# The router's count of preceding tokens: a running sum on VectorE and two products on TensorE instead of one product a unit, with the first stage planned anew

## The chip, the cores and the metric

The kernel runs on one core of a Trainium2 chip. The core has five engines with queues of their own: TensorE (PE in the profile; its weight loads are PEld), VectorE (DVE), ScalarE (ACT), GpSimd (POOL) and SyncE (SP, which here only issues transfers). The metric is device time in microseconds for one execution.

## What is computed

Two layers, one after the other. The first is a DeltaNet attention: 4 batches, 8 heads, 768 positions, head size 48. Each head keeps a 48x48 state and walks along the positions:

```python
k_n = k / (norm(k) + 1e-6)
for t in range(S):
    y[:, :, t] = q_t @ state
    v_old = state.T @ k_t
    state = state + b_t * outer(k_t, v_t - v_old)
```

The result, as 3072 rows of 384, goes into a mixture of 8 experts with a noisy router:

```python
noisy = x @ w_gate + log1p(exp(x @ w_noise)) * noise
top2 = the two largest of 8; weights = softmax over these two
for e in range(8):
    out[rows of e] += weight * (relu(x[rows of e] @ w1[e]) @ w2[e])
```

All numbers are float32; `w1[e]` is 384x1024 and `w2[e]` is 1024x384.

## The kernel before

The first stage (`deltanet`, up to about 356 us in the profile) works in chunks of 64 positions. A unit is one chunk of two batches, 128 rows; a step `s` (0 to 5) is four units (`US`). Within a chunk the recurrence becomes matrix products with the inverse of a triangular matrix. The names that matter:

- `products` (L630, with the transposes L614) makes the Gram matrices of the keys. ScalarE or VectorE copies their diagonal blocks out (L663, L669), and VectorE transposes them (L680).
- `invert` inverts the blocks of one to three steps at once, on VectorE: a scaling (L749), then 30 pairs of column operations (L761 and L765), then a scaling (L777). The groups are `INVERSIONS`: step 0, steps 1 and 2, steps 3 and 4, step 5. `end_inversion` transposes the result (L788, L796), and `join` puts it together with copies on ScalarE (L819, L853, L857) and products (L839, L845).
- `within` makes the masked product of queries and keys, `qk` (L882).
- `recur` and `answer` walk through the units. GpSimd scales `v` (L912), TensorE multiplies keys and state (L630), VectorE subtracts (`v`, L932), TensorE solves (L948), ScalarE copies `u`, TensorE gathers the new state (L970), VectorE adds it (L982); TensorE makes the answer (L903, L1007), which is stored, transposed (L1017) and multiplied with the router's weights (L1022).

The router (`route`) runs three times (`ROUTES`): after step 2 for 12 units, after step 4 for 8, and after step 5 for 4. VectorE finds the two experts of each token; `taken` is a 128 x units x 8 table of zeros and ones. Each token then needs the number of earlier tokens with the same expert, which is its row in that expert's list. `count_earlier` makes this in PSUM: one product with a strictly triangular matrix counts within the unit (L1144), a product with `ones` for each shift by one unit or more adds the preceding units of the run (L1146), and a last one adds `before`, the counts of the preceding runs (L1150). `rows` turns the count into addresses, and `spread` scatters a token's number, weight and place to its list in DRAM, by one indirect transfer per unit and choice on GpSimd (L441). `counted` brings `before` up to date (L1171).

When a part of expert 0's list is there, its rows are gathered (`early_rows`, L1283 and L405) and computed already in the first stage (`early`, L1327 to L1384), for five tiles of 128 rows. Then the expert stage begins: `rest` does what is left of expert 0, and seven experts follow, with products that are saved by sums of blocks (`PLAN`, L1596). This stage is written in a fixed order and isn't touched by the change, but for line numbers.

The order of the first stage is made by a planner when the kernel is built. `Jobs.add` takes each piece of work with its engine, a cost, what it reads and writes, and perhaps a due time; `order` plays the jobs through and takes, engine by engine, among those that could start at about the same moment, the one due first. What comes out is the instruction order of each engine's queue, and it is fixed: at run time an engine waits for the instruction at the head. The constants below bear on this:

- `FIRST`, `PACE`, `BEHIND` give the due times of each step; `SOONER` moves those of `rows`.
- `AFTER` is added to the due time of the scatters, `APART` is their distance.
- `PATIENCE` is how much later a more urgent job may start and still be preferred; `SOON` makes jobs due that hold a PSUM bank.
- `EASY` (one number for each router run) multiplies the time that the planner allows for results of the router's steps to reach another engine (`lands`).

Of the kernel before, what the change touches and what calls it, by code (L numbers as in the profile page):

```python
# [11 lines left out]
ALU = mybir.AluOpType  # L12
ACTF = mybir.ActivationFunctionType
AX = mybir.AxisListType
# [13 lines left out]
EARLY_TILES = 5  # L28
WEIGHTS = 300.0
WITHIN = {}  # L30
EASY = 0.4, 0.4, 0
SOONER = 10, 40, -40
PUT_IN_RULE = -1
ROWS = TILES * 128 + MORE
# [2 lines left out]
ROUTES = [(0, 3), (3, 2), (5, 1)]  # L37


FIRST, PACE, BEHIND = 15, 44, 165  # L40
INVERSIONS = [(0, 1), (1, 2), (3, 2), (5, 1)]


# [57 lines left out]
class Jobs:  # L101
# [45 lines left out]
    def order(self):  # L147
# [28 lines left out]
        while len(done) < len(jobs):  # L176
            first = {}
            best = None
            for engine in self.ENGINES:
# [12 lines left out]
                if at:  # L192
                    soon = min(at)[0] + self.PATIENCE
                    pick = min((x for x in at if x[0] <= soon), key=lambda x: x[1:])
# [7 lines left out]
            if job.opens:  # L202
# [4 lines left out]
                for y in job.opens.users:  # L207
                    if jobs[y].late is None:
                        jobs[y].key = 0, min(jobs[y].due, end + self.SOON)
            if job.closes:  # L210
# [12 lines left out]
                    could[jobs[j].engine].add(j)  # L223
        return sorted(done, key=lambda job: job.start)

    AFTER = 20
    APART = 1.6
    PATIENCE = 0.014
    SOON = 32

    def run(self):

# [5 lines left out]
def kernel(  # L238
# [39 lines left out]
    nc = tc.nc  # L278
# [3 lines left out]
    E = moe_w_gate.shape[1]  # L282
# [22 lines left out]
        out=mask_u, in_=mask_u, pattern=[[1, 128]], base=0, channel_multiplier=-1,  # L305
# [18 lines left out]
    ones = const.tile([128, 128], FP32, name="ones")  # L324
# [20 lines left out]
    before = const.tile([128, E], FP32, name="before")  # L345
# [124 lines left out]
    def deltanet(ictx):  # L470
# [4 lines left out]
        jobs = Jobs(  # L475
            [psum.tile([128, 512], FP32, name=f"single{i}") for i in range(2)],
            [psum.tile([128, 2, 512], FP32, name=f"pair{i}") for i in range(3)],
        )
        PE, ACT, DVE, POOL, SP = Jobs.ENGINES

        def bank(size, ahead=False):

            if size == 2:
                return Bank(2, (0, 1) if ahead else (0, 1, 2))
            return Bank(1, (0,) if ahead else (0, 1))

        def sb(shape, name, dtype=FP32):
            return pool.tile(shape, dtype, name=name)

        def ring(shape, name, n, zero=None, engine=nc.gpsimd):  # L490

            made = [sb(shape, f"{name}{i}") for i in range(n)]
            for t in made:
                for part in zero(t) if zero else ():
                    engine.memset(part, 0.0)
            return lambda i: made[i % n]
# [24 lines left out]
        WIDE = max(x for _, x in ROUTES) * US  # L521
# [550 lines left out]
            for x in ("top0", "top1", "expert0", "expert1", "p1", "den", "row")  # L1072
        }
        metas = ring([128, WIDE, 2, META], "meta", 2)
        r_count = sb([128, E], "r_count")
        slots = [[sb([128, WIDE], f"slot{i}_{x}", I32) for x in range(2)] for i in range(2)]

        def route(g):
# [4 lines left out]
            s, units = first_s + steps - 1, steps * US  # L1083
            u, w, d, noisy, hit0, hit1, taken, at = (x[:, 0:units] for x in full.values())
# [7 lines left out]
            p = bank(1)  # L1092

            def vv(out, a, b, op):
                nc.vector.tensor_tensor(out=out, in0=a, in1=b, op=op)  # L1095
# [46 lines left out]
            def count_earlier():  # L1142
                p_at = p.tile[:, 0 : units * E].rearrange("p (u e) -> p u e", e=E)
                nc.tensor.matmul(p_at, mask_u, taken, start=True, stop=False)  # L1144
                for i in range(1, units):
                    nc.tensor.matmul(  # L1146
                        p_at[:, i:], ones, taken[:, 0 : units - i],
                        start=False, stop=False, skip_group_check=True,
                    )
                nc.tensor.matmul(  # L1150
                    p_at, ones, before[:, None, :].to_broadcast([128, units, E]),
                    start=False, stop=True,
                )

            def rows():
                p_at = p.tile[:, 0 : units * E].rearrange("p (u e) -> p u e", e=E)
# [10 lines left out]
                nc.vector.reciprocal(gate0, den)  # L1167
                vv(gate1, p1, gate0, ALU.mult)

            def counted():  # L1170
                nc.vector.tensor_reduce(  # L1171
                    out=r_count, in_=taken.rearrange("p u e -> p e u"), axis=AX.X, op=ALU.add
                )
                vv(before, before, r_count, ALU.add)

            looked_up = [("early_meta", lo) for x in EARLY if x < first_s for lo, _ in EARLY[x][:1]]
            every_logit = [("logits", g % 2, i) for i in range(units)]
# [11 lines left out]
                writes=[("num", g % 2)],  # L1189
            )  # L1190


            easy = lambda x: x * EASY[g]
            jobs.add(
# [4 lines left out]
                lands=easy(4.0),  # L1199
# [4 lines left out]
                writes=["r_w", "r_noisy"],  # L1204
# [6 lines left out]
                writes=["r_u", "r_hit1", "r_p1", "r_taken"], lands=easy(4.0),  # L1211
            )
            jobs.add(
                PE, 0.3 + 0.28 * units, count_earlier, reads=["r_taken", "before"], opens=p,
                lands=easy(2.0),
            )
            jobs.add(ACT, 0.25, lambda: nc.scalar.activation(p1, p1, ACTF.Exp), writes=["r_p1"])
# [2 lines left out]
                writes=["r_at", "r_d", "r_row", ("slot", g % 2)], closes=p,  # L1220
                due=FIRST + s * PACE + BEHIND - SOONER[g],
            )
            jobs.add(DVE, 0.9, weights, reads=["r_p1"], writes=["r_den", meta])
            jobs.add(DVE, 0.4, counted, reads=["r_taken"], writes=["before"])
            for x in range(units):
                of, i = first_s + x // US, x % US
                for y, to in enumerate(slot):
# [5 lines left out]
                        reads=[("slot", g % 2), meta, ("num", g % 2), "blank", *looked_up],  # L1233
                        writes=[("rows", of, i, y)], lands=2.0, moves=0.2,
                        due=FIRST + (s + paced) * PACE + BEHIND + jobs.AFTER,
                        apart=jobs.APART * paced,
# [197 lines left out]
        for s in range(NS):  # L1434
            units = range(s * US, (s + 1) * US)
            g = inversion_of[s]
            if s == INVERSIONS[g][0]:
# [7 lines left out]
                for x in range(s, s + INVERSIONS[g][1]):  # L1445
                    for j, cost, moves, emit, writes in large.get(x, ()):
                        jobs.add(
                            SP, cost, emit, writes=writes, lands=2.0, moves=moves,
                            reads=[("column", x, j)],
                        )  # L1450
            end_inversion(s)
            if s + 1 == NS:
                jobs.add(
                    SP, 0.7, lambda: nc.sync.dma_start(out=w1_even, in_=w1r[0]), lands=2.0,
                    writes=[
                        "w1", ("t", 0),
                        *(("gd", i, lo) for i in range(US) for lo in range(0, 128, Q)),
                    ],
# [4 lines left out]
                    writes=["w2", ("t", 1)], moves=5.5, due=WEIGHTS + 20.0,  # L1463
# [9 lines left out]
            if s + 1 == sum(ROUTES[turn_r]):  # L1473
                route(turn_r)
# [12 lines left out]
    with ExitStack() as ictx:  # L1487
        weights, early_puts = deltanet(ictx)
# [371 lines left out]
    with tc.If(count > ROWS):  # L1860
        for e in range(E):
            with tc.tile_pool(name=f"left{e}", bufs=1) as pool:
                w1e, w2e = load_weights(weight_tiles(pool), e)
                earlier, added = added, []
                for i in range(TILES, NT):
# [19 lines left out]
                    for fo in range(FT):  # L1885
                        p_h = psum.tile([128, 128], FP32, name="p_hl")
                        for do in range(KT):
                            nc.tensor.matmul(
                                p_h, w1e[:, do, fo * 128 : (fo + 1) * 128], xe[:, do],
                                start=(do == 0), stop=(do == KT - 1),  # L1890
# [40 lines left out]
```

## Time and profile before

| | us |
|---|---|
| three timed runs | 837.17, 839.2, 845.06 |
| median | 839.2 |
| the profiled execution | 798.04 |
| its span, from first to last instruction | 796.2 |

| engine | busy, us | share of the span | instructions |
|---|---|---|---|
| TensorE | 712.5 | 89% | 9361 |
| TensorE weight loads | 559.4 | 70% | 9361 |
| VectorE | 537.6 | 68% | 1079 |
| ScalarE | 309.2 | 39% | 728 |
| GpSimd | 417.6 | 52% | 408 |

The profile is of one execution. Busy shares are averages over two stages that differ, so the text reads windows and chains: the slices cut the span in 40, each digit being the busy tenths of one, and PEclk the clock granted to TensorE in tenths of full speed. The mean granted clock over the whole execution was 0.906. In the chain of waits each line is a start, a duration and the work that ended last. One float32 product of the program is two matmul records.

### The profile page before, as it was taken

To read this page: it belongs to the slowest core of one execution; us is meant where nothing else is said; L and a number is where in the kernel's file an instruction comes from. 1 tells how busy PE (TensorE), PEld (TensorE's weight loads), DVE (VectorE), ACT (ScalarE), POOL (GpSimd) and SP (SyncE) were. 2 spreads that over 40 slices of the span, in tenths; PEclk is the share of its full clock that TensorE was granted. 3 is DMA by queue.
4 is the path that set the end of the run, shared out by engine and by line. 5 is a ranking of instruction groups with operands and counts; after the bars stand their busy time and mean duration, and the time that the engine had idled before them with its cause. 6 is when DMAs were issued, how large, how long until landed. Compare 5 with 4: busy or idle time off the path is not lost.

```text
span 796.2 us, 22454 instructions
## 1 busy us (share of the span) xinstructions
PE 712.5 (89%) x9361; PEld 559.4 (70%) x9361; DVE 537.6 (68%) x1079; ACT 309.2 (39%) x728; POOL 417.6 (52%) x408
## 2 busy tenths in 40 slices
PE   4656878788878889999999999999999999999993
PEld 3445767677768778766597597597596596696693
DVE  7899969999971243016786785785885884884831
ACT  3658387758646432212511511502502602502500
POOL 5021021110255345588886796786787787786032
PEclk8556786977787699999999999999999999999997
DMA  3457553412544213358346346355355345423031
GB/s 66 82 103 191 143 138 78 89 41 60 147 75 122 62 30 127 99 125 165 120 140 130 87 139 133 86 137 126 93 137 118 103 126 118 110 43 42 0 41 25
DMA packets 142719, 79.60 MB, mean 100 GB/s; under 512 B 118352, under 2 KB 139024, under 8 KB 141584
## 3 DMA queue, kind: packets, MB, share of 16 engines
q1 hardware_dynamic: 125840, 57.25, 27.4%
q0 software_dynamic: 12800, 19.80, 13.5%
q8 instruction: 75, 1.23, 0.7%
q10 hardware_dynamic: 3968, 1.03, 0.6%
q14 instruction: 36, 0.29, 0.1%
HBM read 49.85 MB, written 20.03 MB: 88 GB/s over the span
## 4 chain that ended last, share of the span: by engine, by line
PE 66%; DVE 15%; issue 11%; ACT 3%; POOL 3%; SPq 1%; DMA 1%; ACTq 1%; DVEq 0%; POOLq 0%
PE inner L1596 26%; PE outer L1596 14%; DVE w2e L761 4%; PE pair L1348 3%; PE pair L630 3%; PE pair L1372 3%; DVE w2e L765 2%; POOL out_dram L460 2%; PE pair L1007 2%; PE pair L970 2%; PE inner L1707 2%; PE single L1022 2%; PE pair L948 2%; PE single L614 2%; DVE w1e L765 2%
## 5 line engine op out<-in xcount | busy, mean ns | idle before, releaser
L1663 ACT ACTIVATE hT<-inner 128x416 f32<-128x416 f32 x112 | 57.9, 517 | 260.8 <-PE inner L1596 259.4
L1657 DVE TENSOR_TENSOR hT<-hT,inner 128x416 f32<-128x416 f32 x182 | 105.6, 587 | 64.1 <-PE inner L1596 56.0
L460 POOL DMA_INDIRECT out_dram<-sums,metas_x x51 | 83.4, 1635 | 89.8 <-DVE sums L1496 67.3
L912 POOL TENSOR_TENSOR v<-v,norms 128x384 f32<-128x384 f32 x24 | 22.4, 943 | 127.2 <-DVE norms L744 50.0
L1596 PE MATMUL inner<-s_x,w1e 128*128 128x416 f32 x196 | 78.7, 512 | 0.0
L441 POOL DMA_INDIRECT tokens_x<-meta,slot x48 | 47.6, 993 | 38.1 <-DVE r_d L1095 20.2
L405 POOL DMA_INDIRECT xr<-rows_y,metas_x x49 | 56.3, 1150 | 20.4 <-issue 12.7
L1652 ACT ACTIVATE hT<-hT 128x416 f32<-128x416 f32 x112 | 59.9, 547 | 12.1 <-DVE hT L1657 6.5
L1596 PEld LDWEIGHTS inner<-s_x,w1e 128*128 128x128 f32 x196 | 37.2, 190 | 31.2 <-issue 29.0
L1596 PE MATMUL inner<-xe,w1e 128*128 128x416 f32 x140 | 58.1, 513 | 0.0
L1596 PE MATMUL outer<-t_w,hT 128*128 128x192 f32 x336 | 58.0, 326 | 0.0
L1596 PE MATMUL inner<-s_x,s_w 128*128 128x416 f32 x140 | 56.9, 512 | 0.0
L1596 PEld LDWEIGHTS outer<-t_w,hT 128*128 128x128 f32 x336 | 55.2, 190 | 0.0
L1562 POOL TENSOR_TENSOR w1e<-w1e 128x256 f32<-128x256 f32 x63 | 53.5, 859 | 2.3
L1596 PE MATMUL outer<-w2e,hT 128*128 128x192 f32 x280 | 50.7, 328 | 0.3
L1596 PEld LDWEIGHTS outer<-w2e,hT 128*128 128x128 f32 x280 | 46.1, 190 | 4.3 <-issue 2.2
L1596 PEld LDWEIGHTS inner<-s_x,s_w 128*128 128x128 f32 x140 | 26.6, 190 | 22.3 <-issue 22.3
L1596 PEld LDWEIGHTS inner<-xe,w1e 128*128 128x128 f32 x140 | 26.4, 190 | 20.6 <-issue 16.2
L1596 PE MATMUL outer<-t_w,s_h 128*128 128x192 f32 x224 | 40.6, 329 | 0.0
L1492 DVE TENSOR_SCALAR sums<-outer,metas_x 128x192 f32<-128x192 f32 x70 | 27.8, 411 | 18.4 <-PE outer L1596 17.8
L819 ACT COPY w<-tt_tb 32x256 f32<-32x256 f32 x96 | 38.6, 402 | 3.4 <-DVE tt_tb L796 1.7
L1596 PEld LDWEIGHTS outer<-t_w,s_h 128*128 128x128 f32 x224 | 36.6, 190 | 4.2 <-issue 4.2
(203 smaller groups left out, 1568.4 us busy)
## 6 DMA issues: line engine op xcount, KB each, us to landing
w1e<-in_moe_w_dram SPq DMA_DIRECT2D x8, 1536.0 KB
w2e<-in_moe_w_dram SPq DMA_DIRECT2D x8, 1536.0 KB
v<-in_v_dram SPq DMA_DIRECT2D x48, 96.0 KB
qp<-in_q_dram SPq DMA_DIRECT2D x48, 96.0 KB
out_dram<-empty SPq DMA_DIRECT2D x4, 1152.0 KB
rows_y<-y SPq DMA_DIRECT2D x24, 192.0 KB
xq<-xr SPq DMA_DIRECT2D x52, 84.0 KB
kp<-in_k_dram SPq DMA_DIRECT2D x88, 48.0 KB
```

The costliest lines, as they stand in the source:

```text
L405: d = nc.gpsimd.indirect_dma_start(out=got, out_offset=None, in_=rows_y[0 : units * 128], in_offset=bass.IndirectOffsetOnAxis(ap=index, ax ...
L441: d = nc.gpsimd.indirect_dma_start(out=tokens_x, out_offset=bass.IndirectOffsetOnAxis(ap=slot, axis=0), in_=meta, in_offset=None, bounds_c ...
L460: d = nc.gpsimd.indirect_dma_start(out=out, out_offset=bass.IndirectOffsetOnAxis(ap=index, axis=0), in_=got, in_offset=None, bounds_check= ...
L761: v_.tensor_tensor(out=part, in0=t[:, :, j + 1 :, j, None].to_broadcast(shape), in1=t[:, :, None, j, 0:j].to_broadcast(shape), op=ALU.mult,)
L765: columns[:] = [v_.tensor_tensor(out=t[:, :, j + 1 :, 0:j], in0=t[:, :, j + 1 :, 0:j], in1=part, op=ALU.add).ins]
L819: lambda rows=rows, cols=cols, w64=w64, tt=tt: nc.scalar.copy(w64[rows, :, cols], tt[rows]),
L1492: nc.vector.tensor_scalar_mul(got, p, gate)
L1562: engine.tensor_tensor(out=block(to), in0=block(x), in1=block(y), op=ALU.add if sign == "+" else ALU.subtract,)
L1596: nc.tensor.matmul(p, lhsT, rhs, start=opens and i == 0, stop=i == len(products) - 1, skip_group_check=True,)
L1652: nc.scalar.activation(h, h, ACTF.Relu)
L1657: nc.vector.tensor_tensor(out=h, in0=h, in1=p, op=ALU.add if sign > 0 else ALU.subtract)
L1663: nc.scalar.mul(h, p, float(sign))
```

## The change

In `route`, a new job `so_far` on VectorE copies `before` into the first part of a new tile `r_so_far` (128 x 12 x 8), adds the units of `taken` one after the other, each sum into the next part, and the last one into `before`. `count_earlier` keeps the product with the triangular matrix and multiplies `ones` with `r_so_far` in one product. The products for single shifts, the tile `r_count` and the job `counted` are gone. The planner's costs go with it, and five of its constants have new values, so that the whole first stage is ordered anew.

```diff
-EASY = 0.4, 0.4, 0
+EASY = 1, 0.4, 0
...
-FIRST, PACE, BEHIND = 15, 44, 165
+FIRST, PACE, BEHIND = 15, 43, 165
...
-    AFTER = 20
+    AFTER = -20
     APART = 1.6
-    PATIENCE = 0.014
-    SOON = 32
+    PATIENCE = 0.112
+    SOON = 44.8
...
-        r_count = sb([128, E], "r_count")
+        r_so_far = sb([128, WIDE, E], "r_so_far")
...
             def count_earlier():
                 p_at = p.tile[:, 0 : units * E].rearrange("p (u e) -> p u e", e=E)
                 nc.tensor.matmul(p_at, mask_u, taken, start=True, stop=False)
-                for i in range(1, units):
-                    nc.tensor.matmul(
-                        p_at[:, i:], ones, taken[:, 0 : units - i],
-                        start=False, stop=False, skip_group_check=True,
-                    )
-                nc.tensor.matmul(
-                    p_at, ones, before[:, None, :].to_broadcast([128, units, E]),
-                    start=False, stop=True,
-                )
+                nc.tensor.matmul(p_at, ones, r_so_far[:, 0:units], start=False, stop=True)
...
-            def counted():
-                nc.vector.tensor_reduce(
-                    out=r_count, in_=taken.rearrange("p u e -> p e u"), axis=AX.X, op=ALU.add
-                )
-                vv(before, before, r_count, ALU.add)
+            def so_far():
+                nc.vector.tensor_copy(r_so_far[:, 0], before)
+                for i in range(units):
+                    to = r_so_far[:, i + 1] if i + 1 < units else before
+                    vv(to, r_so_far[:, i], taken[:, i], ALU.add)
...
             jobs.add(
-                PE, 0.3 + 0.28 * units, count_earlier, reads=["r_taken", "before"], opens=p,
+                DVE, 0.2 + 0.19 * units, so_far, reads=["r_taken"], writes=["before", "r_so_far"],
+                lands=easy(2.0),
+            )
+            jobs.add(
+                PE, 0.6, count_earlier, reads=["r_taken", "r_so_far"], opens=p,
                 lands=easy(2.0),
             )
...
-            jobs.add(DVE, 0.4, counted, reads=["r_taken"], writes=["before"])
```

## The prediction

> **What bounds the kernel now.** I read the slices first, then the windows by stage, then the chain of waits, and last the instructions of VectorE around the router. In the slices (40 of 19.9 us) the right-hand part is TensorE alone at full clock; the first 15 slices are mixed:
>
> ```profile
> PE   4656878788878889999999999999999999999993
> DVE  7899969999971243016786785785885884884831
> PEclk8556786977787699999999999999999999999997
> ```
>
> Cut at the stages, the columns being busy us (and instructions) of TensorE, weight loads, VectorE, ScalarE, GpSimd, then granted clock, DMA share and GB/s:
>
> ```profile
> 115.00:135.00 20.00, 17.14 (x590) 15.13 (x591) 17.12 (x30) 14.23 (x39) 4.16 (x4) 0.58 0.30 65
> 135.00:165.00 30.00, 23.61 (x985) 20.84 (x985) 28.75 (x48) 21.65 (x55) 4.04 (x4) 1.00 0.42 94
> 165.00:190.00 25.00, 22.46 (x715) 19.93 (x715) 23.59 (x52) 17.18 (x48) 2.93 (x3) 0.73 0.22 51
> 190.00:215.00 25.00, 22.40 (x701) 19.95 (x701) 23.38 (x63) 19.64 (x51) 2.81 (x3) 0.73 0.44 122
> 215.00:275.00 60.00, 49.03 (x1501) 43.73 (x1505) 25.68 (x56) 27.34 (x70) 29.66 (x33) 0.75 0.37 80
> 275.00:300.00 25.00, 21.31 (x762) 19.02 (x756) 9.91 (x38) 11.43 (x30) 9.76 (x11) 1.00 0.15 43
> 300.00:356.00 56.00, 55.48 (x254) 41.93 (x252) 9.27 (x39) 10.92 (x33) 36.08 (x41) 1.00 0.40 120
> ```
>
> Up to 215 us VectorE is full (92.84 of 100 us) and TensorE is not (85.61, so 14.4 us idle); afterwards VectorE is half empty. From 300 us TensorE has no gap. The chain of waits changes engine at 214 us and stays on TensorE, and the router's products lie on it:
>
> ```profile
> 213.35 0.69 DVE qk L882
> 214.05 0.04 issue
> 214.09 0.91 PE pair L903 x46
> ...
> 284.94 1.52 PE single L1146 x14
> ...
> 313.90 0.65 PE single L1146 x6
> ```
>
> VectorE's timeline gives the stretch that ends there: it begins after a wait for ScalarE, and ends with the two `v` subtractions of a recurrence (L932):
>
> ```profile
> 116.25 1.93 DVE L680 STREAM_TRANSPOSE w1e<-w1e 128x1024 f32<-128x1024 f32 x1 [6.01 <-ACT w1e L663]
> 203.72 1.95 DVE L796 STREAM_TRANSPOSE tt_tb<-w1e 128x1024 f32<-128x1024 f32 x1
> 211.75 0.25 DVE L1095 TENSOR_TENSOR r_at<-single,part 128x96 f32<-128x96 f32 x1
> 213.95 1.01 DVE L932 TENSOR_TENSOR v<-v,pair 128x384 f32<-128x384 f32 x2
> ```
>
> So the end is set by VectorE to 214 us and by TensorE after it. The experts (from 373.6 us) aren't touched; what counts is when TensorE gets there.
>
> **The skill.** "TensorE: Matmul & The Clock Gate", section "LDWEIGHTS (loading the stationary operand)": a load costs by the weight's columns, 128/1.2 = 107 ns, however little streams after it. A float32 product has two records here, so 213 ns is the estimate; the chain shows 1.52/7 = 0.217 us. It agrees. "VectorE: DVE Perf Modes", section on the TRN2 errata: a vector instruction pays a fixed latency, so small ones aren't cheap in proportion. Agrees: a 128x8 addition took 198 ns (row below), a 128x96 one 258 to 259 ns. "TensorE: Matmul & The Clock Gate", section "What's actually happening": the clock is half unless recent activity releases it, judged over windows of some 3.4 us. The trace has whole 5 us slices at 0.50 and at 1.00; a block of 32 records of L970 took 1.03 and 0.61 us.
>
> ```profile
> L1095 DVE TENSOR_TENSOR before<-before,r_count 128x8 f32<-128x8 f32 x3 | 0.6, 198 | 0.1
> ```
>
> **The change, part by part.**
>
> Products. Each run of `route` loses its units - 1 products with `ones`: 11, 7 and 3. In TensorE time: 2.39 us (11 x 0.217) near 208 us, 1.52 at 285, 0.65 at 314. The last two, 2.17 us, are on the chain. The two products left were there before.
>
> Vector sums. `so_far` has units + 1 small dependent instructions: 13, 9 and 5. I take 0.22 us each (198 ns and the gap): 2.9, 2.0 and 1.1 us. Removed, by their rows: 0.52, 0.43 and 0.42 us of `counted`. But the sums stand ahead of the product, `counted` stood behind everything. At run 0 the product took 3.0 us (207.4 to 210.4), now 2.9 plus some 0.6: the latency is a draw. At run 1 `r_taken` was finished at 281.15 and its product began at 284.57, a slack of 3.4 us against 2.0 of sums; at run 2 311.42 and 313.76, 2.3 against 1.1. Behind the product on TensorE's in-order queue all the recurrences wait, so if that slack were gone it would cost its whole lateness, up to 3.1 us together. I take 0.
>
> Plan: VectorE's order. Up to about 193 us it is nearly the old one. Then the new order puts the four operands that TensorE needs (two `qk` of L882, two `v` of L932) directly behind `so_far`, and the inversion of the last step behind those. Ahead of the second `v` there stood 17 pairs of columns (L761, L765) of that inversion, now 10. The seven moved (220, 228, 234, 238, 240, 240, 238 elements) took 0.79 to 0.88 us by their starts, together 5.95 us. The seven instructions of `rows` (211.75 to 213.35, 1.6 us) and the three of `weights` (0.54) move behind it too. Against that 2.9 us are added: 5.95 + 1.6 + 0.54 - 2.9 = 5.2 us earlier. The postponed inversion ended at 238.05 us, its first product on TensorE came at 256.2: 18 us of cover, of which 7 are used.
>
> Plan: ScalarE's order. VectorE's 6.01 us wait ended with the last L663 copy of the products of steps 3 and 4. ScalarE was full from 109 to 116 us. Nine L819 copies into `w` stood between the end of the inversion (106.6) and that copy, now five: 4 x 0.41 = 1.6 us earlier, unless TensorE is late with the product that the copy reads (then 0).
>
> So VectorE delivers its last operand 5.2 + 1.6 = 6.8 us earlier. TensorE can follow: to 215 us it had 14.4 us idle, and loses 2.39 us of work. I take all 6.8; the lower bound is TensorE's own 2.39, in case its gaps come back elsewhere.
>
> Plan: GpSimd, SP and the tail. GpSimd has the same instructions, with the route-0 scatters (L441) and `v` scalings (L912) in another order; the scatters ended at 266.5, the rows that need them were turned on TensorE at 289.4, so nothing comes of it. SP's queue keeps its long transfers (weights, `metas_x`). For the second early batch the gathers were issued at 313.7 and 315.05; with the 3 us to landing of the neighbouring gathers that is about 318 to 319, and TensorE turned those rows at 322.6: slack 4 us. The work on TensorE from the end of run 1's count to there, counted in the two orders, falls by 0.8 us (32.9 to 32.1), most of it run 2's products: the slack holds. The last rows were gathered by 346.0 and wanted at 355.9: it holds too.
>
> Sum: 6.8 + 2.17 = 9.0 us. The profiled execution took 798.04 us (span 796.2 and 1.8 around it): 789.0. The three timed runs have a median of 839.2, 1.052 times that, an excess the trace doesn't explain; I scale with it: 9.0 x 1.052 = 9.4, so **829.8 us**, 1.1% faster.
>
> **Rivals.**
>
> A, the lead is not used: TensorE's gaps before 214 us are waits on ScalarE and stretches that the profile calls "issue" (over 1 us each), and an earlier operand doesn't close them. Then only products count: 2.17 to 4.56 us, at 1.052 2.3 to 4.8: 834.4 to 836.9, no change to speak of. For it: TensorE was busy 22.4 of the last 25 us before 215. Against: 14.4 us idle over the 100.
>
> B, slower, by the clock. The place is 135 to 165 and 275 to 300 us, where TensorE ran at 1.00 though busy only 23.61 of 30 and 21.31 of 25. If the rearranged waits let both fall to 0.50, the busy time grows by the ratio of the L970 blocks, 1.03/0.61 = 1.7: 16.5 and 14.9 us more, less the idle it fills (6.4 and 3.7) gives 10.1 + 11.2 = 21.3. Less 9.0: 12.3 slower, at 1.052 **852 us**. It decides from 9.0 us of clock loss on, about one of the two stretches lost whole. For it: the clock changes between these levels all through 15 to 280 us. Against: less waiting should keep it up.
>
> C, the clock rises: of 215 to 275 us at 0.75, half is cold. If 20 us of that goes to full clock, busy time falls by 20 x (1 - 1/1.7) = 8 us beyond the forecast: 821 us.
>
> D, the count is later than its slack, for the vector sums or the POOL chain behind it: 3 us lost, 833 us. The edit doing nothing at all is excluded by the two orders.
>
> **Chances and range.** Forecast 0.40 (own range 825 to 833), C 0.17, A and D 0.25, B 0.18. Within 1% (831 to 847.6) is about what a measurement of this kernel can tell from no change, the three runs spreading from 837.17 to 845.06. Faster by over 1%: the forecast and C, 0.57; within: 0.25; slower: 0.18. The range goes from 816 (C with a longer stretch) to 846 (half of B): **816 to 846**.
>
> **What would show it.** Right: the second `v` of that recurrence ends by 208 to 211 us instead of 214.95; VectorE's 6 us wait near 116 is shorter; L1146 is gone, and TensorE doesn't wait for `r_so_far` at a count; the experts' first `inner` product starts near 365 instead of 373.6. Wrong: that start unchanged, or TensorE waiting for VectorE at a count, or a mean granted clock in 115 to 300 us that differs by more than 0.05 from the old one, which would settle the time by itself.

## The result, and the profile after

The changed kernel took 829.74 us (median of 4 runs, 829.14 to 832.93), the kernel before, beside it, 840.81 us: ratio 0.988, interval [0.9842, 0.9919]. The forecast was 829.8 us. Two later runs, each on a chip of its own, agree: 0.9891 [0.9857, 0.9925] and 0.9895 [0.9841, 0.9948]. Times are medians of all executions; ratios leave out the slow ones, over 1.5% above the fastest of their kernel.

The number is right; the path to it is right in part only. The profiled execution of the changed kernel took 829.14 us, that of the kernel before 798.04 us: by the traces alone the change would seem to cost 31 us. The page after, in 40 slices of 20.7 us:

```profile
PE   5656879898887875999999999999999999999993
DVE  7999968998762240302588488487586686785831
...
PEclk8556886987575775999999999999999999999997
```

TensorE is now weak in the second half of the first stage (slices 13 to 16, the last at 5 tenths). The same windows as before (busy us and, in brackets, instruction records of TensorE, weight loads, VectorE, ScalarE, GpSimd; granted clock, DMA share, GB/s):

```profile
190.00:215.00 25.00, 21.50 (x673) 18.92 (x664) 21.66 (x67) 14.13 (x36) 1.66 (x2) 0.70 0.36 87
215.00:275.00 60.00, 49.49 (x1252) 41.84 (x1252) 25.91 (x57) 25.95 (x66) 27.01 (x27) 0.59 0.36 87
275.00:300.00 25.00, 21.40 (x697) 18.40 (x693) 12.49 (x48) 12.42 (x33) 5.83 (x8) 0.80 0.17 51
300.00:356.00 56.00, 42.76 (x412) 34.58 (x413) 10.31 (x44) 9.99 (x28) 25.20 (x27) 0.79 0.23 76
```

From 300 to 356 us TensorE is busy 42.76 us instead of 55.48. VectorE's timeline around the first run of the router, from the wait at 115 us to the second `v` (in brackets the idle time before, and what ended it):

```profile
114.97 1.94 DVE L680 STREAM_TRANSPOSE w1e<-w1e 128x1024 f32<-128x1024 f32 x1 [5.32 <-ACT w1e L663]
```

```profile
196.18 2.10 DVE L788 STREAM_TRANSPOSE tt_tb<-w1e 128x1024 f32<-128x1024 f32 x1 [1.90 <-PE single L845]
...
205.58 0.16 DVE L1163 COPY r_so_far<-before 128x8 f32<-128x8 f32 x1
205.78 2.17 DVE L1095 TENSOR_TENSOR r_so_far<-r_so_far,r_taken 128x8 f32<-128x8 f32 x11
207.99 0.17 DVE L1095 TENSOR_TENSOR before<-r_so_far,r_taken 128x8 f32<-128x8 f32 x1
...
209.27 0.55 DVE L932 TENSOR_TENSOR v<-v,pair 128x384 f32<-128x384 f32 x1
209.74 1.92 DVE L796 STREAM_TRANSPOSE tt_tb<-w1e 128x1024 f32<-128x1024 f32 x1
211.51 0.53 DVE L932 TENSOR_TENSOR v<-v,pair 128x384 f32<-128x384 f32 x1
```

The 13 sums take 2.58 us, and the second `v` ends at 212.04 us instead of 214.96: 2.9 us earlier. But the two traces come from different levels of time. What makes one and the same order take 798 or 840 us had to be found before the 1.2% could be placed.

### The profile page after: what moved, and what is told of

Its sections match the earlier page's. It is cut to its first block, busy times and chain, and to the rows that moved or that the text cites. A ratio compares the mean times of both kernels' runs of the same rounds, so it can differ in the third digit from the quotient of the medians.

```text
span 827.3 us, 22382 instructions
## 1 busy us (share of the span) xinstructions
PE 732.1 (88%) x9319; PEld 572.1 (69%) x9319; DVE 541.8 (65%) x1100; ACT 308.6 (37%) x728; POOL 418.5 (51%) x408
## 4 chain that ended last, share of the span: by engine, by line
PE 65%; DVE 15%; issue 11%; POOL 3%; ACT 2%; SPq 2%; DMA 1%; another core or an unknown queue 0%; POOLq 0%; DVEq 0%; ACTq 0%
PE inner L1591 25%; PE outer L1591 14%; DVE w2e L761 5%; PE pair L1343 3%; PE pair L1367 3%; PE pair L630 3%; DVE w1e L765 3%; POOL out_dram L460 2%; DVE w2e L765 2%; PE pair L903 2%; PE inner L1702 2%; PE single L1022 2%; PE pair L948 2%; PE pair L1007 2%; PE pair L970 1%
## 5 line engine op out<-in xcount | busy, mean ns | idle before, releaser
L441 POOL DMA_INDIRECT tokens_x<-meta,slot x48 | 48.5, 1010 | 63.4 <-DVE w2e L765 25.9
L405 POOL DMA_INDIRECT xr<-rows_y,metas_x x49 | 55.7, 1138 | 19.1 <-issue 12.8
L1591 PEld LDWEIGHTS inner<-s_x,s_w 128*128 128x128 f32 x140 | 26.6, 190 | 22.3 <-issue 22.3
L1591 PEld LDWEIGHTS inner<-xe,w1e 128*128 128x128 f32 x140 | 26.4, 190 | 20.7 <-issue 17.0
```

The lines of the kernel that those rows point to most:

```text
L405: d = nc.gpsimd.indirect_dma_start(out=got, out_offset=None, in_=rows_y[0 : units * 128], in_offset=bass.IndirectOffsetOnAxis(ap=index, ax ...
L441: d = nc.gpsimd.indirect_dma_start(out=tokens_x, out_offset=bass.IndirectOffsetOnAxis(ap=slot, axis=0), in_=meta, in_offset=None, bounds_c ...
L1591: nc.tensor.matmul(p, lhsT, rhs, start=opens and i == 0, stop=i == len(products) - 1, skip_group_check=True,)
```

## The experiments

**The kernel before, once more, and each part alone.** The kernel unchanged:

> The kernel before, unchanged, for a second profile. Its profiled execution took 798 us and its timed runs 837 to 845; the profiled execution of the changed kernel took 829 like its timed runs. Theory 1 (the trace of 798 us is an ordinary execution, the extra 41 us of the timed runs lies outside the span): a span near 796 us again and a time near 798. Theory 2 (the same program executes in two ways): a span of 836 to 843 us, with the experts taking their 58.5 us each as before and 40 us more between 200 and 330 us, on TensorE, in gaps between matmuls of one block.

It took 802.36 us, with a span of 800.5 us; the kernel before had a median of 800.89 us (795.01 to 808.78) on this chip. So a trace holds the whole time, and in these runs the level goes with the chip: 801 us on this one, 839 to 843 us on the three chips of the later experiments (the first, second and third slower chip below), and 840.81 us beside the changed kernel's first runs. (Each chip was used once, so that it is the chip and nothing else of the hour is likely, not shown.)

The new count in the old order (the sums are emitted ahead of the products, in the old place of the product):

```diff
             def count_earlier():
                 ...
+                so_far()
                 nc.tensor.matmul(p_at, mask_u, taken, start=True, stop=False)
-                for i in range(1, units):
-                    ...
+                nc.tensor.matmul(p_at, ones, r_so_far[:, 0:units], start=False, stop=True)
...
             def counted():
-                ...
+                pass
```

> The kernel before with the old costs and constants of the planner, so with its old order; only what is emitted changes: the job of the count emits the running sum on VectorE and then the two products, and the job of the old counts emits nothing. Theory 1 (the lead of VectorE comes from the new order, 6.8 us, and the products give 2.2 us on the chain after 214 us): 837 to 839 against 840.8 before, so 2 to 5 us of the 11. Rival (the whole gain is in TensorE's instructions): 829 to 831. Rival (the sums delay VectorE by 4 us in its full stretch): 841 to 845.

The changed kernel with the old products put back behind its sums:

```diff
                 nc.tensor.matmul(p_at, mask_u, taken, start=True, stop=False)
-                nc.tensor.matmul(p_at, ones, r_so_far[:, 0:units], start=False, stop=True)
+                for i in range(1, units):
+                    nc.tensor.matmul(p_at[:, i:], ones, taken[:, 0 : units - i], ...)
+                nc.tensor.matmul(p_at, ones, r_so_far[:, 0:1].to_broadcast([128, units, E]), ...)
```

> The changed kernel in its own order, with so_far as it is, but the count made by the old products: one with the triangular matrix, one with ones for each shift, and one with the first part of r_so_far. 21 products of TensorE more, all else equal. Theory 1: the order's gain stays, 2.2 to 4.6 us of products come back: 832 to 835. Rival (all in the products): 839 to 841.

The kernel before with the five constants alone (`EASY`, `PACE`, `AFTER`, `PATIENCE`, `SOON`):

> The kernel before with the five new constants of the planner (EASY, PACE, AFTER, PATIENCE, SOON) and the old code and costs. Theory 1 (an order that puts the operands of TensorE ahead of the last inversion is worth 6.8 us): 832 to 836. Rival (the constants fit the new costs alone): 838 to 850.

All three ran on the chip at 801 us, so of the expected times only the distances to the kernel before can be compared:

| kernel | time, us | ratio to before | second `v` ends |
|---|---|---|---|
| before | 800.89 | | 215.75 |
| new count, old order | 802.9 | 1.0015 [0.999, 1.004] | 219.73 |
| new order and sums, old products | 800.19 | 0.9979 [0.9958, 1.0] | 212.62 |
| constants alone | 799.24 | 0.9982 [0.9962, 1.0003] | 211.69 |

A second `v` that ends 3.1 or 4.1 us earlier goes with 0.2% less there, and both intervals reach no change. One that ends 4.0 us later goes with 0.15% more, again with no change inside the interval. The step "TensorE can follow; I take all" doesn't hold at this level: even the lower ends of the first two intervals are only 0.4% below, some 3 us. (Each `v` is of one trace.)

**The changed kernel and the kernel before on the first slower chip, both with a trace.**

> The changed kernel as it is, beside the kernel before on this chip, whatever the level of this chip is. In the earlier runs with the kernel before near 801 us the single parts moved it by 0.2% or less. Theory 1 (the 1.2% belongs to the change as a whole: new order and cheap products together): ratio 0.985 to 0.992 here too, second v of L932 ending near 208 to 212 us. Theory 2 (the 1.2% was had in a stretch in which TensorE's records come in bursts, from 245 to 322 us, and belongs to that chip): if this chip runs the kernel before near 801 us, the ratio is 0.996 to 1.003; if it runs it near 840 us, 0.985 to 0.992.

> The kernel before once more, for a trace on the same chip as the trace of the changed kernel. Both theories: if its time is near 840 us, its first inner product (L1596) starts near 405 instead of 374 us, and the lost 30 us show as issue time of TensorE between 245 and 325 us where GpSimd has L441 scatters back to back. If its time is near 800 us, the start is near 375 us.

They took 830.57 us (ratio 0.9891 [0.9857, 0.9925]) and 839.93 us. At this level both theories expected the same ratio, so this tells them no further apart; but now both traces are of one chip, and by TensorE's timeline the three counts divide the time:

| us | before, profile shown first | before, first slower chip | changed, first slower chip |
|---|---|---|---|
| count of run 1 ends | 286.7 | 304.4 | 299.3 |
| count of run 2 begins | 313.6 | 352.8 | 346.1 |
| first `outer` of the rest of expert 0 | 355.2 | 395.0 | 387.6 |
| span | 796.2 | 838.1 | 829.2 |

Of the 41.9 us between the levels, 17.7 are lost before run 1's count has ended and 21.5 between it and run 2's. What follows takes nearly the same time (2.7 us more). TensorE's timeline of the kernel before, in that stretch of the first slower chip ("issue": the engine waited for nothing that the profile shows):

```profile
307.60 1.29 PE L630 MATMUL pair<-qT,kT 64*64 64x64 f32 x20
309.14 0.51 PE L630 MATMUL pair<-qT,kT 64*64 64x64 f32 x5 [0.24 <-issue]
309.91 0.48 PE L630 MATMUL pair<-qT,kT 64*64 64x64 f32 x4 [0.27 <-issue]
310.65 0.26 PE L630 MATMUL pair<-qT,kT 64*64 64x64 f32 x1 [0.26 <-issue]
...
326.33 0.26 PE L630 MATMUL pair<-qT,kT 64*64 64x64 f32 x1 [1.62 <-issue]
327.05 0.37 PE L630 MATMUL pair<-qT,kT 64*64 64x64 f32 x2 [0.45 <-issue]
327.76 0.26 PE L630 MATMUL pair<-qT,kT 64*64 64x64 f32 x1 [0.34 <-issue]
328.46 0.71 PE L630 MATMUL pair<-qT,kT 64*64 64x64 f32 x12 [0.44 <-issue]
```

These are two blocks of 32 matmul records (16 products each); in the chain of the profile shown first such a block took 0.5 to 1.0 us. From 309 us on they come one to five at a time, most at steps of 0.7 or 1.4 us, for 19 us (lines left out are of the same kind, with a few of L1017 and L1327). GpSimd meanwhile issues the 16 scatters (L441) of run 1 back to back, the first at 305.62 and the last at 324.99 us. TensorE isn't alone. ScalarE's and VectorE's timelines (of the same execution) have waits that end with nothing the profile can name ("remote": no releaser was found on this core):

```profile
306.82 0.17 ACT L1053 COPY logits<-single 128x16 f32<-128x16 f32 x1 [0.88 <-PE single L1022]
328.58 0.48 ACT L1045 COPY xT<-single 128x384 f32<-128x384 f32 x1 [21.59 <-remote]
```

```profile
311.39 0.56 DVE L982 TENSOR_TENSOR st<-pair,st 128x384 f32<-128x384 f32 x1 [5.47 <-remote]
```

The `xT` copy takes what the L1017 products wrote; the last of these ended at 313.41 us, and the copy started 15 us later, when the scatters were over. The trace of the kernel before that was shown first has not one such "remote" wait on these engines between 200 and 400 us. Windows of 22 us over the 16 scatters of run 1 (columns as above), first the kernel before on the chip at 801 us, then on the first slower chip, then the changed kernel there:

```profile
287.00:309.00 22.00, 20.06 (x382) 17.62 (x382) 3.65 (x12) 6.66 (x19) 15.78 (x16) 0.77 0.12 31
```

```profile
305.00:327.00 22.00, 10.94 (x109) 7.53 (x104) 1.72 (x8) 0.65 (x2) 15.78 (x16) 0.50 0.06 11
```

```profile
300.00:322.00 22.00, 8.68 (x110) 7.23 (x102) 2.60 (x8) 0.96 (x2) 15.78 (x16) 0.66 0.04 6
```

GpSimd's 15.78 us in 16 instructions are the same in all three. Beside the same scatters TensorE gets 382 matmul records done on one chip and 109 or 110 on the other. The DMA engines are nearly idle (a share of 0.04 to 0.12), so it isn't the amount of data moved.

The Trainium skill, "DMA: Bandwidth & Descriptors", section "SWDGE vs HWDGE vs iDMA", says that GpSimd writes the descriptors of its transfers to rings in SBUF by software, and names VectorE as what can hold GpSimd up there. The trace shows the other direction: GpSimd keeps its pace, and the others are late. "Perfetto Trace Analysis", section "Summary: the profiler window per engine type", says that the profile's window of an instruction leaves out how its semaphore reaches the others. That agrees with what is seen: the loss stands in no instruction's duration, only in gaps marked "issue" and "remote". Whether the semaphores or the instructions come late isn't shown.

**Without the scatters of run 1.** The tokens of this run are then missing from the experts' lists, and so from the result. In both kernels:

```diff
                         lambda x=x, of=of, y=y, to=to: [
                             spread(metas(g)[:, x, y], to[:, x : x + 1], of, columns)
-                        ],
+                        ] if g != 1 else [],
```

> The kernel before without the 16 scatters (L441) of the second routing run: these tokens are not handed to the experts, so their rows are left out of the result, and later gathers move fewer bytes. Theory 1 (scatters don't slow TensorE): first inner product within 2 us of the kernel before on the same chip. Theory 2 (TensorE's stream slows beside scatters): on a chip at 840 us the start comes 10 to 20 us earlier, at 800 us 2 to 5 us earlier, and the issue time of TensorE at 115 to 330 us falls.

> The changed kernel without the same 16 scatters of the second routing run (these tokens are left out of the result). Theory 1 (the change's gain lies in VectorE's order to 214 us): the same distance to the kernel before without them as between the full kernels. Theory 2 (the gain lies beside the scatters): the two kernels without these scatters are within 0.3% of each other.

They took 817.13 us (0.9742 [0.9698, 0.9786] of the kernel before) and 810.07 us (0.9653 [0.9608, 0.9698]): 22.3 us less than the kernel before with them, and 20.5 us less than the changed kernel. Kernel before without them:

```profile
300.00:330.00 30.00, 28.46 (x539) 24.82 (x534) 10.28 (x45) 10.79 (x31) 3.02 (x3) 1.00 0.45 152
```

With them this stretch had 18.11 busy us in 176 matmul records at a clock of 0.50. From the end of run 1's count to the start of run 2's it takes 25.5 us (before) and 25.3 us (changed) without the scatters, 48.4 and 46.8 us with them. So these 16 scatters cost some 22 us on that chip; fewer rows are gathered later, but the difference stands in this stretch. This is the whole of the second loss in the table. The first (17.7 us, 215 to 300 us, beside the 24 scatters of run 0) has such a wait too (5.60 us of VectorE, "remote", up to 255.43 us), but no run left those out.

Between the two kernels 7.1 us remain without them (four executions each, 814.46 to 820.56 and 808.44 to 814.14 us), against 8.9 us with them. Most of the gain doesn't come from the stretch beside run 1's scatters: the kernels differ there by 1.6 us with them and 0.2 without.

**Large products in that stretch.** If only small products were slowed, the early experts' large ones could be put there:

```diff
             job.key = (0, job.due) if job.due < 1e8 else (1, job.late or 0.0)
+            if job.late is not None and job.late < 1.0:
+                job.key = (0, 300.0 + job.late)
```

> The changed kernel with one more edit to the planner: the early experts of the first batch (turned rows, L1343 and L1367, 8 + 8 products of 1.2 us planned) are given a rank ahead of all other work, so that TensorE has them right after the second routing run's count, while GpSimd issues that run's 16 scatters; the recurrences' small products come behind. Nothing is left out. Theory 2 (on a chip at 840 us, TensorE issues small products at one to five in 0.7 us while those scatters are issued, and loses some 16 us of 302 to 323 us; large products need few instructions): on such a chip 12 to 18 us faster than the changed kernel, that is ratio 0.968 to 0.976 to the kernel before. On a chip at 801 us: within 3 us of the changed kernel. Theory 1 (scatters slow TensorE whatever it does, or the loss is a wait for data): within 3 us of the changed kernel on either chip, or slower.

> The changed kernel as it is, again on whatever chip this is. At the 840 us level: ratio 0.985 to 0.992 to the kernel before, as twice so far. At the 801 us level it has not been run. Theory 1 (the gain is in VectorE's order to 214 us and holds on any chip): ratio 0.988 to 0.993 there. Theory 2 (the gain is had where small products stand beside scatters, and is that chip's): 0.996 to 1.004 there.

On the second slower chip the changed kernel took 830.37 us (0.9895 [0.9841, 0.9948]); with the experts first it was 842.03 us (831.18 to 846.66), 0.9991 [0.9946, 1.0036] of the kernel before. The expected 12 to 18 us did not come; by the ratios it is slower than the changed kernel by about 1.0%. The chip was at 840 us, so the changed kernel has not been run at 801 us. TensorE's timeline with the experts first, in an execution of 843.72 us (the added lines move L1343 to L1345):

```profile
301.30 1.56 PE L1345 MATMUL pair<-early_xe,w1e 128*128 128x256 f32 x6
302.70 0.81 PE L1024 MATMUL single<-wgn,xT 128*128 128x16 f32 x6
309.78 5.55 PE L1345 MATMUL pair<-early_xe,w1e 128*128 128x256 f32 x18 [6.27 <-issue]
322.18 7.47 PE L1345 MATMUL pair<-early_xe,w1e 128*128 128x256 f32 x24 [6.85 <-ACT tt_tb L1356]
329.49 10.48 PE L1369 MATMUL pair<-w2e,tt_tb 128*128 128x384 f32 x32
```

Large products do come without gaps, 18 records in 5.55 us at a clock of 0.74 (12 took 2.75 us in the profile shown first, at 1.00). But each block hands its PSUM bank to ScalarE, and ScalarE is late as well. Its first two copies of them and the one between:

```profile
312.56 0.38 ACT L1356 ACTIVATE tt_tb<-pair 128x256 f32<-128x256 f32 x1 [11.00 <-remote]
317.52 0.17 ACT L1055 COPY logits<-single 128x16 f32<-128x16 f32 x1 [4.57 <-remote]
321.75 0.94 ACT L1356 ACTIVATE tt_tb<-pair 128x256 f32<-128x256 f32 x3 [4.06 <-remote]
```

So TensorE stands still for 6.27 and 6.85 us, and the small products that were put behind come later: run 2's count begins at 364.7 us, in the changed kernel on the same chip at 350.5. The idea fell on this: that TensorE needs few instructions doesn't help as long as what it hands to ScalarE is taken up late.

**Each part alone, on the third slower chip.** The kernels with the constants alone and with the new count alone again:

> The kernel before with only the five constants of the planner changed (its old count and old products): on a chip at 801 us it had a ratio of 0.9982. If this chip runs the kernel before near 840 us: Theory 1 (the order of VectorE and of the other queues makes the gain) 0.987 to 0.993; Theory 2 (the cheap products make it, by shortening what stands ahead of the second run's scatters) 0.996 to 1.003. Near 801 us: 0.996 to 1.000 as before.

> The changed count alone (sums on VectorE, two products for a run) in the order of the kernel before: on a chip at 801 us it had a ratio of 1.0015. If this chip runs the kernel before near 840 us: Theory 1 (the order makes the gain) 0.998 to 1.006; Theory 2 (the products make it) 0.988 to 0.994. Near 801 us: 0.999 to 1.004 as before.

Both stand still: 842.09 us, 0.9994 [0.9969, 1.0019], and 842.34 us, 1.0003 [0.9976, 1.0031], beside 842.68 us. On this chip each theory is contradicted by one of them: the constants alone don't make the gain, and the new products in the old order don't. On VectorE the second `v`, first with the constants alone, then with the new count alone:

```profile
215.20 0.55 DVE L932 TENSOR_TENSOR v<-v,pair 128x384 f32<-128x384 f32 x1
```

```profile
218.98 1.01 DVE L932 TENSOR_TENSOR v<-v,pair 128x384 f32<-128x384 f32 x2
```

It ends at 215.75 and 219.99 us, in the kernel before on the first slower chip at 214.94, in the changed one at 210.91 to 213.96 (three traces). Neither the whole change nor a trace of the kernel before was taken on this third chip: the whole was faster by 1.1% on other chips, its parts not at all on this one.

## Why the prediction was right, point by point

**What bounds the kernel.** "From 300 us TensorE has no gap" was true of the profile shown and not of the timed runs. Their excess, "which the trace doesn't explain", was 42 us in two places before 353 us. Scaling 9.0 us by 1.052 had no ground: the excess is a sum, not a factor. It cost only 0.4 us of forecast. The two profiled executions can't be compared either: the experts' first `inner` product came at 404.5 us, not near 365, and the first `outer` at 386.1 instead of 355.2. On the first slower chip, the one with both traces, the first `outer` came 7.4 us earlier (387.6 for 395.0).

**The sums.** 13 instructions, 2.58 us measured for 2.9 foreseen; TensorE nowhere waits for `r_so_far`. Right, as was the value of the slack at runs 1 and 2.

**The products.** Foreseen 2.17 us on the chain, from 0.217 us each. On the first slower chip the chain of the kernel before shows this at run 1's count:

```profile
300.33 0.62 PE single L1144 x2
300.94 2.89 PE single L1146 x14
303.84 0.52 PE single L1150 x2
```

and 0.65 us at run 2's: 3.54 us together. At run 1's count the granted clock was 0.50, at run 2's 1.00. The whole count of run 1 took 4.10 us (300.26 to 304.36) and takes 0.66 us, that of run 2 1.20 and 0.52. So 4.1 us of the 8.9 between the two spans stand at the counts themselves, 1.9 of them because of the clock of this one execution: in the two other traces of slower chips with the old products (without run 1's scatters, and with the constants alone) the clock was 1.00 there and L1146 took 1.52 us, as foreseen. The term was right as it stood; what it gave beyond that in this trace is chance.

**The lead of VectorE.** ScalarE's copies gave 1.3 us for 1.6 (the transpose L680 began at 114.97, not 116.25; 1.0 us in the pair on the first slower chip). The rest came in part: 6.8 us were foreseen, 2.9 measured between the two profiles shown and 4.0 on the first slower chip. Behind `r_taken` the new order gave 4.8 us in both pairs; what is missing was lost ahead of it. The step that failed is "up to about 193 us it is nearly the old one": with the earlier start, and with two of the seven moved pairs gone from in front of it, `r_taken` should have been ready earlier, and was ready later, at 205.67 instead of 203.8 us (204.52 for 203.76 on the first slower chip). VectorE was busy for 21.66 of the 25 us from 190, not 23.38, and a new wait of 1.90 us for the products of L845 ends at 196.18. The interval of 208 to 211 us held in one trace of the changed kernel in three.

**All of it taken by TensorE.** On the 801 us chip rival A, the lead unused, describes the runs: 3.1 or 4.1 us earlier goes with 0.2%. On the first slower chip run 1's count began 1.6 us earlier (298.63 for 300.26), though `v` was 4.0 us earlier; without run 1's scatters, 1.7 us earlier (301.15 for 302.87) with a `v` 3.9 us earlier. The windows before had shown room to lose a lead: from 215 to 275 us TensorE was busy 49.03 of 60 us. In the other two traces of the changed kernel the count began at 297.47 and 303.23 us, so traces of different chips don't settle 1.6 us. What is left of the 8.9 us, some 3.1, stands between the end of run 1's count and the start of run 2's (1.6) and after the first `outer` (1.5); between run 2's count and `outer` there is nothing. No run tells what made these.

**The parts alone.** The new count alone in the old order saves the same products, but its sums lie in VectorE's way: the second `v` ends at 219.99 us, for 214.94 in the kernel before on the first slower chip, and TensorE waits 0.69 us for `r_so_far` at run 0's count. The two nearly cancel, and run 1's count ends at 304.69 us for 304.36. In the new order the second `v` isn't later but earlier, sums included. This is argued from traces of different chips, not shown by a run of its own. Of the constants alone it says only that their `v` was not earlier on the third slower chip (215.75), while on the chip at 801 us it was, with the same program. And a rival stands untested: the whole change ran on the first and second slower chip, its parts on the third and on the chip at 801 us. That nothing of it would gain on those two isn't excluded, so that the gain needs both parts isn't shown.

**The clock.** By my own rule a mean granted clock that differs by over 0.05 from 115 to 300 us would have settled the time: it was 0.80 in the profile before and 0.72 in the one after, which by the rule spoke against the forecast. But the two profiles were of different levels; on the first slower chip it is 0.75 and 0.75, so rivals B and C didn't happen there.

**The slack of the tail.** It held: in the changed kernel on the first slower chip the last early rows' gathers were issued at 335.07 to 337.74 us, and TensorE turned them at 354.30 without a wait.

In sum, by the pair of traces with all scatters: 4.1 us from the counts where 2.2 were foreseen, a lead of 4.0 where 6.8 were foreseen, of which some 1.6 is seen at run 1's count, and 3.1 us that no step named. The pair without run 1's scatters has 2.0 us from the counts, 1.7 at run 1's count and 0.5 behind: 4.2 between the spans. That the 8.9 us between the first two agree with the 9.0 foreseen is luck: most of the lead was lost, and the clock of one execution and unnamed time made up for it. Whether the change gains on a chip at 801 us is open: no run of it was made there.

## What to carry to other kernels

Compare traces of one chip before reading a difference: here the same program took 801 or 840 us, and the trace shown was of the other level than the times. A wait with no releaser on several engines at once, while one queue runs at its own pace, points to that queue; leaving its work out tells what it costs. Try an edit and the order it needs together: in the old order TensorE waited 0.69 us for the sums, in the new one not at all. And run the whole beside its parts on one chip; here that was not done.

## What was not expected of the hardware

- Beside back-to-back scatters of GpSimd (1.29 us apart) three of four chips let TensorE, ScalarE and VectorE take up work up to 15 us late. On the one of these where they were left out, 16 scatters cost some 22 us. On the fourth, TensorE was busy 20.06 of 22 us beside the same scatters. What differs between the chips isn't known.
- Gathers didn't show it: beside nine L405 gathers from 363.64 to 375.05 us the changed kernel on the first slower chip kept TensorE busy 23.73 of 24 us from 356 to 380. There it ran large products only, so this is the weaker evidence.
